# Decoding float64 weights: the sign by a Sign activation and a multiplication instead of a bit operation

## The chip, the cores and the metric

The kernel runs on one core of a Trainium2 chip, as one launch. Times are device microseconds (us) of that core, from the first instruction to the last result in memory. A profiled execution of each kernel gives a trace of every instruction. The engines are called PE (matrix multiplication), DVE (VectorE), ACT (ScalarE), POOL (GpSimd) and SP (which issues most transfers).

## The reference

Three stages follow one another. The first is attention with only the 32 largest scores of each row kept, over 4 batches, 8 heads, 576 positions, head size 64. The second is a feed-forward layer with softplus on 2304 tokens of 512, hidden size 2048. The third sends each token to one of 8 experts.

```python
scores = scale * np.matmul(q, k.transpose(0, 1, 3, 2))
kth = np.partition(scores, -top_k, axis=-1)[..., -top_k:-top_k + 1]
scores = np.where(scores >= kth, scores, -1000000000.0)
...
h = x @ w_in                                   # w_in: 512 x 2048, float64
g = np.maximum(h, 0.0) + np.log1p(np.exp(-np.abs(h)))
x = (g @ w_out).astype(np.float32)             # w_out: 2048 x 512, float64
...
expert_idx = np.argmax(x @ w_gate, axis=1)
ye = np.maximum(xe @ w1[e], 0.0) @ w2[e]       # per expert, scaled by its gate
```

The weights `w_in` and `w_out` of the second stage arrive as float64. The engines compute in float32, so the kernel has to decode them: each value is two 32-bit words, and the float32 is made from both.

## The kernel before

`part_one` does attention and the feed-forward layer, `part_two` the experts. Attention is cut into 72 groups of two score tiles of 128x576. For a group, PE makes the scores (line 394), ACT copies them (402), DVE finds the 32nd largest value by folding the row and by rounds of MAX and MATCH_REPLACE (430 to 454), ACT takes the exponential (443), the exponentials are multiplied by a mask (on POOL, 466, with the mask from DVE, 465; from group 12 on one of the two tiles is masked on DVE alone, 462), ACT makes a 16-bit copy (470), POOL subtracts to get the remainder (471, 472), a DMA transposes the result, and PE multiplies it by v three groups later (489, 491).

Once a tile of tokens has all its heads, the feed-forward layer takes it in units of up to two tiles, in 16 steps per unit: a first layer (576), the exponential and logarithm on ACT (590, 591), and a second layer (616). `some_work` starts 1.7 such steps per group, as far as units are ready.

The weights are decoded in 32 steps of 128x512 values, 16 of `w_in` and 16 of `w_out`, by `decode` (from line 225). Two steps are called ahead of group 0 and four behind each softmax, at the lowest priority; the scheduler that writes the order of every engine places them between the other work, so that they spread over some 20 groups. A step loads the words into `w` (two buffers), of which `hi` and `lo` are views with a stride of two words. With the buffer `a` (called `xr` in the trace, two buffers, shared with a later use) it does:

- line 233, ACT: the high word, read as a float, times 2 to the power of -111, into `a`;
- line 235, DVE: `a` shifted left by 3 bits, in place, which puts exponent and upper mantissa where a float32 has them, and drops the sign;
- line 237, ACT: the low word as an integer, scaled and rounded to the lowest bits, in place;
- line 238, DVE: the sign bit of the high word, or-ed into `a`;
- line 239, POOL: an integer addition of the low bits to `a`, into the target: `t` for `w_in`, `w_out_s` for `w_out`.

For `w_in`, ACT then makes a 16-bit copy of `t` (244, 245) and POOL the remainder (246). PE's first layer waits for these.

Of the kernel before, what the change touches and what calls it, by code (L numbers as in the profile page):

```python
# [8 lines left out]
F32 = mybir.dt.float32  # L9
F32R = mybir.dt.float32r  # L10
F16 = mybir.dt.float16
I32 = mybir.dt.int32
U32 = mybir.dt.uint32
AF = mybir.ActivationFunctionType
ALU = mybir.AluOpType
# [176 lines left out]
def part_one(tc, ctx, q, k, v, w_in, w_out, const, ident, before, ones, iota_e, reg_e, wg, ids,  # L192
             ohcum, done, early, table, rows, flags, sums, w_sums, e_sums):
    nc = tc.nc
# [30 lines left out]
    def decode(src, kk, c0, dst):  # L225
        w = dec.tile([128, 2 * C], I32, name="w", bufs=DWB)
        nc.sync.dma_start(w, src[:, kk, 2 * c0:2 * (c0 + C)])
        w = w.rearrange("p (a b) -> p a b", b=2)
        hi, lo = w[:, :, 1], w[:, :, 0]
        a = x2p.tile([128, ROWW], F32, name="xr")[:, :C]  # L230


        nc.scalar.activation(a, hi.bitcast(F32), AF.Copy, scale=2.0 ** -111)
        u = a.bitcast(U32)
        nc.vector.tensor_scalar(u, u, 3, None, op0=ALU.logical_shift_left)

        nc.scalar.activation(lo, lo.bitcast(U32), AF.Copy, scale=2.0 ** -29)
        nc.vector.scalar_tensor_tensor(u, hi.bitcast(U32), 0x80000000, u, op0=ALU.bitwise_and, op1=ALU.bitwise_or)  # L238
        nc.gpsimd.tensor_tensor(out=dst.bitcast(I32), in0=a.bitcast(I32), in1=lo, op=ALU.add)

    def decode_w_in(kk, j):
        t = dec.tile([128, C], F32, name="t")
        decode(w_in_v, kk, j * C, t)
        nc.scalar.activation(w_in_s[:, kk, j, 1], t, AF.Abs, accum_out=w_sums[:, j, kk:kk + 1])
        nc.scalar.activation(w_in_s[:, kk, j, 0], t, AF.Copy)
        nc.gpsimd.tensor_tensor(out=w_in_s[:, kk, j, 1], in0=t, in1=w_in_s[:, kk, j, 0], op=ALU.subtract)
# [39 lines left out]
    for j in range(DFF // C):  # L286
        if flags is None:
            dec_q += [(decode, w_in_v, kk, j * C, w_in_f[:, kk, j]) for kk in range(KD)]
            dec_q += [(split_w_in, j)]
        else:  # L290
            dec_q += [(decode_w_in, kk, j) for kk in range(KD)]
        dec_q += [(decode, w_out_v, kk, c0, w_out_s[:, kk, c0:c0 + C])
                  for kk in range(j * C // 128, (j + 1) * C // 128) for c0 in range(0, DM, C)]
# [791 lines left out]
```

## Time and profile before

| what | us |
|---|---|
| median of 3 runs | 1109.52 (1106.35 to 1110.75) |
| time of the profiled execution | 1105.04 |
| span of the profiled execution | 1103.2 |
| PE busy | 891.7 (81%) |
| DVE busy | 937.9 (85%) |
| ACT busy | 743.3 (67%) |
| POOL busy | 521.4 (47%) |

"Busy" is the time between an instruction's start and its end in the trace. It includes time in which a started instruction waits inside the engine. Idle time before an instruction is listed with the engine or transfer that ended it. The shares are means over the whole span; the stages differ a good deal, so the tables by window matter more than the mean.

### The profile page before, as it was taken

The numbers are of one execution on the slowest core, as the hardware profiler recorded it, in microseconds if no ns is written. First come the engines' busy times: TensorE is split into PE (matmuls) and PEld (weight loads), VectorE is DVE, ScalarE is ACT, GpSimd is POOL, SyncE is SP. The second block draws the span as 40 slices with busy tenths as digits, with TensorE's granted clock in tenths as the row PEclk, the third lists the DMA queues.
The fourth block names the chain that finished last, engine by engine and source line by source line (L and its number), as shares of the span: only waits on it lengthen the run. The fifth ranks groups of instructions, "written<-read, shape, count | busy, mean of one in ns | idle before, by whom it ended". The sixth has DMA issues, their size and how long they took to land.

```text
span 1103.2 us, 22060 instructions
## 1 busy us (share of the span) xinstructions
PE 891.7 (81%) x7146; PEld 648.0 (59%) x7146; DVE 937.9 (85%) x2989; ACT 743.3 (67%) x1738; POOL 521.4 (47%) x571
## 2 busy tenths in 40 slices
PE   1123259757978898799999898998999999999995
PEld 0012135434654564566556565666678899999994
DVE  4998999999977997999899999999746897777774
ACT  5757678777756776767787776775578655555553
POOL 2877988786535564654655554644301011211111
PEclk9998569858889999899999999999999999999998
DMA  7887698876656779644878645434621376566660
GB/s 178 207 155 169 159 202 162 186 184 128 117 94 104 138 123 155 134 78 81 143 147 141 106 91 83 85 76 75 176 67 30 98 249 210 206 245 236 219 230 24
DMA packets 295858, 156.96 MB, mean 142 GB/s; under 512 B 257524, under 2 KB 257652, under 8 KB 295732
## 3 DMA queue, kind: packets, MB, share of 16 engines
q1 hardware_dynamic: 292116, 145.73, 60.4%
q0 software_dynamic: 3616, 9.72, 2.5%
q8 instruction: 58, 0.95, 0.4%
q14 instruction: 68, 0.56, 0.2%
HBM read 77.89 MB, written 11.11 MB: 81 GB/s over the span
## 4 chain that ended last, share of the span: by engine, by line
PE 40%; DVE 27%; DMA 13%; issue 6%; ACT 5%; POOL 5%; SPq 3%; POOLq 0%; ACTq 0%; DVEq 0%
PE h L916 9%; PE y L929 9%; PE h L576 8%; DVE mx L454 6%; DVE wk L450 6%; PE y L616 5%; DMA pT<-p 5%; PE y L613 3%; DVE wk L446 2%; DVE mk L465 2%; DVE e L462 2%; POOL p L472 2%; DVE xr L238 2%; DMA kt<-st 2%; DMA qn<-in_q_dram 2%
## 5 line engine op out<-in xcount | busy, mean ns | idle before, releaser
L576 PE MATMUL h<-xT,w_in_s 128*128 128x256 f16 (+1 forms) x1920 | 227.2, 269 | 27.2 <-ACT sa L590 13.0
L616 PE MATMUL y<-w_out_s,g 128*128 128x512 f32 x480 | 233.2, 607 | 9.3 <-ACT g L591 9.3
L576 PEld LDWEIGHTS <-w_in_s 128*128 128x128 f16 x1920 | 173.6, 101 | 95.5 <-issue 63.6
L394 PE MATMUL s<-kt,q 128*128 128x512 f16 (+7 forms) x640 | 103.6, 327 | 137.1 <-DVE wk L446 90.5
L454 DVE MAX8 mx<-wk 128x8 f32<-128x144 f32 (+2 forms) x432 | 199.0, 495 | 0.1
L466 POOL TENSOR_TENSOR e<-e,mk 128x576 f32<-128x576 f32 x84 | 110.3, 1316 | 130.1 <-DVE mk L465 57.2
L472 POOL TENSOR_TENSOR p<-e,p 128x512 f16<-128x512 f32 x144 | 167.7, 1165 | 0.0
L470 ACT ACTIVATE p<-e 128x576 f16<-128x576 f32 x144 | 97.8, 679 | 94.4 <-DVE e L462 36.5
L394 PEld LDWEIGHTS <-q 128*128 128x128 f16 (+1 forms) x640 | 46.4, 110 | 190.6 <-DVE wk L446 76.7
L450 DVE MATCH_REPLACE8 wk<-mx,wk 128x144 f32<-128x144 f32 (+1 forms) x432 | 144.7, 341 | 0.1
L616 PEld LDWEIGHTS y<-w_out_s,g 128*128 128x128 f32 x480 | 82.2, 192 | 71.3 <-issue 55.2
L916 PEld LDWEIGHTS h<-xT,wf 128*128 128x128 f32 x864 | 111.8, 191 | 5.3 <-ACT wf L877 0.2
L916 PE MATMUL h<-xT,wf 128*128 128x256 f32 x864 | 113.9, 283 | 0.0
L929 PE MATMUL y<-wf,hT 128*128 128x512 f32 x432 | 112.9, 399 | 0.3 <-DVE ds L673 0.3
L443 ACT ACTIVATE e<-s,bias 128x576 f32<-128x576 f32 x144 | 105.0, 767 | 4.6 <-POOL p L472 2.9
L489 PE MATMUL m<-v,pT 128*128 128x65 f16 (+1 forms) x1440 | 96.4, 203 | 13.1 <-ACT xtail L517 5.8
L896 POOL DMA_INDIRECT out_dram<-ot,idx x19 | 19.6, 1029 | 176.1 <-DVE ot L895 173.4
L489 PEld LDWEIGHTS <-pT 128*128 128x128 f16 (+1 forms) x1440 | 89.5, 108 | 18.6 <-issue 14.7
L402 ACT ACTIVATE s<-s 128x1152 f32<-128x1152 f32 x72 | 80.4, 1117 | 11.3 <-PE s L394 11.2
L471 POOL TENSOR_TENSOR p<-e,p 128x64 f16<-128x64 f32 x144 | 51.0, 354 | 76.6 <-ACT p L470 74.4
L929 PEld LDWEIGHTS y<-wf,hT 128*128 128x128 f32 x432 | 76.7, 189 | 13.4 <-DVE ds L673 0.3
L491 PE MATMUL m<-v,pT 128*128 128x64 f16 (+1 forms) x800 | 78.5, 203 | 0.0
(197 smaller groups left out, 1752.5 us busy)
## 6 DMA issues: line engine op xcount, KB each, us to landing
w1r<-in_moe_w_dram SPq DMA_DIRECT2D x20, 1024.0 KB, 4.9
w2r<-in_moe_w_dram SPq DMA_DIRECT2D x20, 1024.0 KB, 7.6
w<-in_moe_w_in_dram SPq DMA_DIRECT2D x16, 512.0 KB, 5.0
w<-in_moe_w_out_dram SPq DMA_DIRECT2D x16, 512.0 KB, 4.0
rows<-xr SPq DMA_DIRECT2D x37, 128.2 KB, 2.5
qn<-in_q_dram SPq DMA_DIRECT2D x16, 288.0 KB, 4.5
kn<-in_k_dram SPq DMA_DIRECT2D x16, 288.0 KB, 3.0
vn<-in_v_dram SPq DMA_DIRECT2D x16, 288.0 KB, 4.5
```

Source lines behind the costliest of these rows:

```text
L394: last_qk[0] = nc.tensor.matmul(ps[p0:p1, base + k0 * D:base + k1 * D], lhsT=lhs, rhs=kt[:, k0:k1, cs], start=first, stop=not first)
L443: nc.scalar.activation(e[i], s[i], AF.Exp, bias=bt[:, i], scale=SCORE if flags is not None else sc[i][:, 3:4])
L450: nc.vector.match_replace(out=to, in_to_replace=mx[:, i, 8 * j:8 * j + 8], in_values=src[i], imm_value=NEG)
L454: nc.vector.max(out=mx[:, i, 8 * j + 8:8 * j + 16], in_=src[i])
L466: nc.gpsimd.tensor_tensor(out=e[i], in0=e[i], in1=mk, op=ALU.mult)
L470: nc.scalar.activation(p16[:, 0:S], e[i], AF.Copy)
L472: nc.gpsimd.tensor_tensor(out=p16[:, S + D:], in0=e[i][:, 0:S - D], in1=p16[:, 0:S - D], op=ALU.subtract)
L489: nc.tensor.matmul(o[:, h, 0:D + 1], lhsT=pT(r), rhs=v16[:, h, c, 0:D + 1], start=r == 0, stop=r == R - 1)
L576: nc.tensor.matmul(hps[:, :n], lhsT=w_in_s[:, c, j, p, o:o + 128], rhs=xT[:, 0:len(u.tiles), r, c, :], start=m == 0, stop=m == 3 * KD - 1)
L616: nc.tensor.matmul(u.y[i], lhsT=g[:, cs], rhs=w_out_s[:, f, :], start=f == 0, stop=f == KF - 1)
L916: nc.tensor.matmul(h, lhsT=w1f[:, a, c, :], rhs=xT[:, b, c, :], start=n == 0, stop=n == 3 * KD - 1)
L929: nc.tensor.matmul(y[i], lhsT=hT[g][:, a, i * 128:i * 128 + 128], rhs=w2f[:, b, :], start=g == 0 and n == 0, stop=g == KF2 - 1 and n == 2)
```

## The change

Line 233 takes the magnitude (Abs) in place of a copy, a new ACT instruction turns the high word into its sign as a float (-1 or 1), in place, the addition writes to `a`, and a second POOL instruction multiplies `a` by the sign into the target. The DVE instruction of line 238 is gone. From line 238 on, line numbers are one higher: 239 is the addition, 240 the multiplication, 238 the Sign.

```diff
-        nc.scalar.activation(a, hi.bitcast(F32), AF.Copy, scale=2.0 ** -111)
+        nc.scalar.activation(a, hi.bitcast(F32), AF.Abs, scale=2.0 ** -111)
         u = a.bitcast(U32)
         nc.vector.tensor_scalar(u, u, 3, None, op0=ALU.logical_shift_left)
 
         nc.scalar.activation(lo, lo.bitcast(U32), AF.Copy, scale=2.0 ** -29)
-        nc.vector.scalar_tensor_tensor(u, hi.bitcast(U32), 0x80000000, u, op0=ALU.bitwise_and, op1=ALU.bitwise_or)
-        nc.gpsimd.tensor_tensor(out=dst.bitcast(I32), in0=a.bitcast(I32), in1=lo, op=ALU.add)
+        nc.scalar.activation(hi.bitcast(F32), hi.bitcast(F32), AF.Sign)
+        nc.gpsimd.tensor_tensor(out=a.bitcast(I32), in0=a.bitcast(I32), in1=lo, op=ALU.add)
+        nc.gpsimd.tensor_tensor(out=dst, in0=a, in1=hi.bitcast(F32), op=ALU.mult)
```

The scheduler writes a new order for every engine. On POOL, at softmax groups 6 and 7 (`e` are the exponentials, `mk` the masks, `p_...` the 16-bit copies of one tile), the order was before:

```order
L466 TENSOR_TENSOR e<-e,mk 128x576 x2
L471 TENSOR_TENSOR p_1075<-e,p_1075 128x64
L472 TENSOR_TENSOR p_1075<-e,p_1075 128x512
L239 TENSOR_TENSOR t<-xr,w 128x512
L471 TENSOR_TENSOR p_1081<-e,p_1081 128x64
L472 TENSOR_TENSOR p_1081<-e,p_1081 128x512
L246 TENSOR_TENSOR w_in_s<-t,w_in_s 128x512
L239 TENSOR_TENSOR t<-xr,w 128x512
L466 TENSOR_TENSOR e<-e,mk 128x576
L246 TENSOR_TENSOR w_in_s<-t,w_in_s 128x512
L466 TENSOR_TENSOR e<-e,mk 128x576
```

And with the change, at the same two groups:

```order
L467 TENSOR_TENSOR e<-e,mk 128x576
L239 TENSOR_TENSOR xr<-xr,w 128x512
L240 TENSOR_TENSOR t<-xr,w 128x512
L467 TENSOR_TENSOR e<-e,mk 128x576
L472 TENSOR_TENSOR p_1101<-e,p_1101 128x64
L473 TENSOR_TENSOR p_1101<-e,p_1101 128x512
L247 TENSOR_TENSOR w_in_s<-t,w_in_s 128x512
L472 TENSOR_TENSOR p_1107<-e,p_1107 128x64
L473 TENSOR_TENSOR p_1107<-e,p_1107 128x512
L467 TENSOR_TENSOR e<-e,mk 128x576
L240 TENSOR_TENSOR t<-xr,w 128x512
L467 TENSOR_TENSOR e<-e,mk 128x576
```

Where a group had two decoding steps between its subtractions, there is now about one per group, and it is two instructions, which stand between the group's multiplications by the mask.

On DVE, the last decoding step stood before in softmax group 19 (`wk` and `mx` are the row being searched and its largest values):

```order
L450 MATCH_REPLACE wk<-mx,wk 128x144 x2
L235 TENSOR_SCALAR xr<-xr 128x512
L515 RECIPROCAL rc<-rc 64x2
L454 MAX mx<-wk 128x8 x2
L238 SCALAR_TENSOR_TENSOR xr<-w,xr 128x512
```

With the change it stands at the end of group 24, ahead of the first line of group 25:

```order
L466 TENSOR_SCALAR mk<-s,mx 128x576
L463 SCALAR_TENSOR_TENSOR e<-s,mx,e 128x576
L235 TENSOR_SCALAR xr<-xr 128x512
L604 TENSOR_TENSOR w<-w_out_s,w 128x512
L431 TENSOR_TENSOR s<-s 128x288
```

The 32 steps now reach five groups further. In ACT's order, counted by the score copies (402) issued ahead of it, the feed-forward layer's 12th step came after 17 groups and now comes after 19, the 24th after 26 and now 28, the 36th after 32 and now 35, the 48th after 38 and now 40, the 96th after 59 in both. ACT's orders hold one load of an activation table each, at the start. The number of transfers is the same.

## Rows read from the trace of the kernel before

**Rows 1.** Page, part 2: busy tenths of 40 slices, PE, DVE and POOL.

```profile
PE   1123259757978898799999898998999999999995
...
DVE  4998999999977997999899999999746897777774
...
POOL 2877988786535564654655554644301011211111
```

**Rows 2.** Windows of the span; columns start:end, length, then busy us (instructions) by engine.

```profile
42.00:176.00 134.00, 52.78 (x467) 34.10 (x468) 129.53 (x358) 94.61 (x194) 113.99 (x106) 0.81 0.82 176
176.00:262.00 86.00, 62.37 (x482) 37.46 (x481) 82.13 (x233) 67.56 (x158) 64.38 (x63) 0.78 0.80 173
262.00:307.00 45.00, 35.20 (x307) 24.11 (x306) 44.83 (x165) 31.46 (x69) 25.77 (x31) 0.85 0.65 120
307.00:440.00 133.00, 112.59 (x921) 72.31 (x920) 110.49 (x395) 87.87 (x215) 67.75 (x77) 0.96 0.73 120
440.00:765.00 325.00, 300.19 (x2721) 200.19 (x2722) 309.85 (x1131) 236.34 (x587) 174.37 (x207) 0.98 0.59 104
765.00:1103.00 338.00, 322.10 (x2230) 277.41 (x2228) 236.06 (x646) 199.91 (x470) 55.89 (x57) 0.99 0.50 164
```

**Rows 3.** Line L238 and, up to 308 us, line L430: xcount, duration ns min/median/max, first and last.

```profile
L238 DVE SCALAR_TENSOR_TENSOR xr<-w,xr x32: 662/1316/1754, 11.0 to 256.9; 128x512 uint32<-128x512 uint32 x32
...
L430 DVE TENSOR_TENSOR s<-s x26: 436/450/467, 22.9 to 306.5; 128x288 f32<-128x288 f32 x26
```

**Rows 4.** Waits of DVE, 42 to 176 us: us in total, times, longest.

```profile
DVE xr L235 <- ACT xr L233: 3.2, 3, 1.6
DVE s L430 <- ACT s L402: 1.2, 1, 1.2
```

**Rows 5.** Timeline, 105.9 to 110 us, DVE and POOL: start, us, engine, line.

```profile
105.95 0.68 DVE L238 SCALAR_TENSOR_TENSOR xr<-w,xr 128x512 uint32<-128x512 uint32 x1
107.11 1.57 DVE L238 SCALAR_TENSOR_TENSOR xr<-w,xr 128x512 uint32<-128x512 uint32 x1
...
106.98 1.16 POOL L472 TENSOR_TENSOR p<-e,p 128x512 f16<-128x512 f32 x1
108.10 1.73 POOL L239 TENSOR_TENSOR t<-xr,w 128x512 int32<-128x512 int32 x1
```

**Rows 6.** Duration of one, lines L235, L446, L239 and L472: xcount, ns min/median/max.

```profile
L235 DVE TENSOR_SCALAR xr<-xr x32: 401/604/1514, 10.5 to 256.0; 128x512 uint32<-128x512 uint32 x32
...
L446 DVE TENSOR_TENSOR wk<-s x72: 740/748/751, 24.7 to 765.1; 128x576 f32<-128x576 f32 x72
...
L239 POOL TENSOR_TENSOR t<-xr,w x16: 1275/1290/1809, 11.8 to 235.2; 128x512 int32<-128x512 int32 x16
...
L472 POOL TENSOR_TENSOR p<-e,p x144: 1147/1159/1367, 37.8 to 777.3; 128x512 f16<-128x512 f32 x144
```

**Rows 7.** Groups of instructions by line and form: busy us, mean ns, idle before.

```profile
L238 DVE SCALAR_TENSOR_TENSOR xr<-w,xr 128x512 uint32<-128x512 uint32 x32 | 38.6, 1205 | 0.1
L235 DVE TENSOR_SCALAR xr<-xr 128x512 uint32<-128x512 uint32 x32 | 24.9, 778 | 7.9 <-ACT xr L233 7.9
...
L239 POOL TENSOR_TENSOR t<-xr,w 128x512 int32<-128x512 int32 x16 | 22.5, 1408 | 10.3 <-DVE xr L238 10.0
...
L233 ACT ACTIVATE xr<-w 128x512 f32<-128x512 f32 x32 | 21.3, 665 | 27.8 <-DMA w<-in_moe_w_in_dram 12.2 <-DMA w<-in_moe_w_out_dram 11.7 <-POOL e L466 2.9
```

**Rows 8.** Windows with line L238 alone: 42 to 176, 176 to 262, and their sum.

```profile
42.00:176.00 134.00, 18.78 (x16) 0.81 0.82 176
176.00:262.00 86.00, 14.57 (x12) 0.78 0.80 173
...
sum 265.00, DVE 33.35; mean DVE 11.12
```

**Rows 9.** Window of 20 us in which POOL was fullest, and the first 42 us.

```profile
0.00:42.00 42.00, 6.44 (x24) 2.39 (x24) 25.00 (x67) 25.55 (x50) 19.25 (x32) 1.00 0.80 185
...
120.00:140.00 20.00, 4.45 (x43) 2.66 (x44) 20.00 (x54) 12.48 (x24) 18.82 (x17) 0.56 0.75 169
```

**Rows 10.** Waits of POOL, 42 to 176 us, the longest.

```profile
POOL p L471 <- ACT p L470: 6.6, 6, 2.6
POOL e L466 <- DVE mk L465: 5.6, 12, 0.8
```

**Rows 11.** Chain of waits, 324 to 328 us, PE: one step of the first unit.

```profile
324.78 1.72 PE y L616 x4
326.50 1.31 PE h L576 x12
```

**Rows 12.** Groups by line: the one table load of ScalarE.

```profile
L95 ACT ACT_TABLE_LOAD x1 | 1.3, 1283 | 0.8 <-PEq L1067 0.8
```

## The prediction, made before the changed kernel was run

> **What bounds the kernel now.** I first read the busy slices of the page [rows 1]. They show three stages: from about 40 to 300 us DVE is full while PE is far from full; from 300 to about 770 us both are near full; after that PE is full. The change is in the first stage only, since line L238 runs from 11.0 to 256.9 us [rows 3]. So the second view is a table of windows, with cuts at the last decoding steps: between 42 and 307 us DVE is busy 129.53 + 82.13 + 44.83 = 256.5 of 265 us, POOL 113.99 + 64.38 + 25.77 = 204.1, ACT 94.61 + 67.56 + 31.46 = 193.6 [rows 2]. The end at 307 is the start of softmax group 25 (line L430 starts its 26th group, counted from 0, at 306.5) [rows 3]; the new order issues the last decoding step there, so it is the place where both kernels have done the same work. The third view, the waits of DVE, says who releases whom: from 42 to 176 us DVE waits 3.2 and 1.2 us for others and for nothing else worth a row [rows 4]. Read alone, that makes DVE the bound, and any DVE work taken away a gain.
>
> The fourth view corrects this. L238 lasts from 662 to 1754 ns, median 1316 [rows 3], for one shape. In the timeline the one at 105.95 us, with no POOL instruction running, takes 0.68 us; the one at 107.11 takes 1.57, and POOL's L472 runs until 108.14 beneath it, so that it ends 0.54 us after L472. POOL's next, an L239, starts at 108.10 and takes 1.73 us [rows 5] where its shortest is 1.275 [rows 6]. So these two engines hold each other up: DVE's "busy" hides waiting for POOL. L235 shows it too (401 to 1514 ns); L446, of which one operand lies in PSUM, does not (740 to 751) [rows 6]. The work that passes through one gate in this stage is POOL's, plus some DVE instructions.
>
> **The change, part by part.** *Removed:* 32 L238, 38.6 us of DVE, mean 1205 ns [rows 7]; 28 of them, 33.35 us, lie after 42 us [rows 8]. Own work in that is 28 x 0.662 = 18.5 us; the rest, 14.8, is waiting. DVE's demand up to group 25 falls to 256.5 - 33.35 = 223.1 us at most, and L235 and L465 will wait longer if POOL is fuller.
>
> *Added on POOL:* 32 float multiplications of 128x512, 28 of them in the stretch. No row shows this one. Below it stands L472 (float, one operand of 16 bits, 1147 shortest, 1159 median), above it the mean of L239, 1408, which has its own holds in it [rows 6, 7]. I take L239's median, 1290, since it has the same tiles, two operands of 4 bytes and one of them with a stride: 28 x 1.29 = 36.1 us, bounds 28 x 1.16 = 32.5 and 28 x 1.408 = 39.4.
>
> *Relief on POOL:* an L238 held the next POOL instruction up by 1.73 - 1.275 = 0.455 us [rows 5, 6]. Bounds: 0 and 28 x 0.455 = 12.7 us. As more than half of the L238 last twice their shortest time, most met a POOL instruction; I take two thirds, 8.5 us. So POOL's demand up to group 25 is 204.1 + 36.1 - 8.5 = 231.7 us (bounds 224 and 243.5), more than DVE's 223.1. POOL becomes the fuller engine.
>
> The Trainium skill (SBUF — State Buffer, "Who interferes with whom") says that a DVE instruction with two SBUF inputs contends with GpSimd reads, and in a two-port mode whichever comes first keeps the shared pair for the whole instruction, the other blocking fully. For who contends, the trace agrees. If the hold were the whole L238, the relief would be 28 x 0.662 = 18.5 us and POOL's demand 221.7; the row above shows 0.455, and the sum goes by that.
>
> *Added on ACT:* 32 Sign activations of the shape of L233, 665 ns [rows 7]: 28 x 0.665 = 18.6 us, ACT to 212 of 265, 80%. I cost it at nothing, since ACT would still have 53 us idle. Without that cover it reaches POOL through the copies L470, for which POOL already waits 6.6 us between 42 and 176 [rows 10]. Abs for Copy on L233 and the addition written to `xr` change no shape: nothing.
>
> *The added wait:* the multiplication stands on POOL behind the addition and waits for the Sign. Queued behind it are the softmax's e-multiplication and the p-subtractions, and after them the transposes, the L470 copies and DVE's next mask (two `mk` buffers). The `w` and `xr` buffers, two each, are held one multiplication longer, 1.29 us and its place in the queue; no load is added, but SP issues them with it. The order spreads the steps over five more groups, which covers this; without that cover it is 28 x 1.29 / 2 = 18 us.
>
> *The first 42 us:* POOL is busy 19.25 of 42 us [rows 9]; four steps lose an L238 and gain a multiplication in its place: nothing.
>
> **The sum.** What share of its time can POOL be busy? In the long dense stretch it was 113.99 of 134 us, 85.1% [rows 2]; in its fullest 20 us 18.82, 94% [rows 9]. I take 85.1%, because POOL's waits there, for L470 and for the mask [rows 10], are still there: 231.7 / 0.851 = 272.3 us instead of 265, **+7.3 us**. The ends: 231.7 / 0.94 = 246 (-19), and 243.5 / 0.851 = 286 (+21).
>
> *Behind group 25* the first-layer steps are late: by the new order the 12th and 24th are issued two groups later, the 36th three, the 96th at the same group. Three groups are some six steps of 1.31 + 1.72 = 3.03 us of PE [rows 11], 18 us, to be fitted into PE's idle time from 307 to 765 us, (133 - 112.6) + (325 - 300.2) = 45 us [rows 2]. Bounds 0 and 18; since the idle time is two and a half times that, I take **+2 us**. Together +9.3 on the profiled execution's 1105.0 us gives 1114.3; the median of the runs shown, 1109.5, stands 4.5 above that execution, so the forecast is **1119 us**.
>
> **Rivals.**
> - *DVE was the bound and POOL keeps up* (the other side). For it: DVE is 97% busy and hardly waits [rows 2, 4], and 33.35 us go. Against it: 14.8 us of those were waiting for POOL, and POOL's load grows. It decides if POOL can run at 94% through the whole stretch, as in its best 20 us: -19 us, 1090. With DVE at 223.1 us and no waits it would be -33 at the very most. Chance 0.23.
> - *Even exchange:* POOL at 87 to 89% (231.7 / 0.88 = 263), because DVE, relieved, delivers masks earlier; or the hold was a whole L238, as the page's rule has it: 221.7 / 0.851 = 260.5, -4.5, with +2 behind: 1107. Between 1104 and 1115. Chance 0.27.
> - *The late steps are not absorbed:* PE is 92% busy from 440 to 765 us, 300.19 of 325 [rows 2], so all 18 us could come out at the end on top of the 7: 1109.5 + 25 = 1135. Chance 0.07.
> - *Sign needs another table:* a load is 1283 ns [rows 12]; two for each of 32 steps are 82 us of ACT, above 1150. Against it: both orders hold one load, at the start. Chance 0.02.
>
> **How the numbers follow.** My forecast has 0.41, its own range 1115 to 1136. What lies within 0.5%, about what a measurement of this kernel can tell from no change, is 1104 to 1115. Slower: 0.41 + 0.07 + 0.02 = 0.50; same 0.27; faster 0.23. The range reaches down to the first rival's price, 1091, beyond which some 0.08 is left, and up to 1138, which takes in the third rival and most of the upper bound (1109.5 + 21 + 2 = 1132), with some 0.08 beyond.
>
> **What would show it.** Right: POOL above 225 us busy up to the 26th L430 and that one later than 307 us; L235's mean above its 778 ns; DVE with idle time that ends on POOL or on ACT's L470; the multiplication near 1.29 us. Wrong: the 26th L430 before 300 us with POOL at 90% or more; a multiplication near 0.9 us; DVE still full; or a group 25 on time and a late end.

## The result, and the profile after

The changed kernel takes 1115.57 us, median of 12 runs (1111.35 to 1118.61), against 1106.88 us for the kernel before, also 12 runs (1101.63 to 1110.75). The ratio is 1.0072, 95% interval 1.0049 to 1.0094: slower by some 8 us, and the interval leaves out no change. The forecast was 1119 us and slower. The profiled execution took 1116.81 us, 11.8 us more than that of the kernel before (1105.04); a comparison of the two traces has these 11.8 us to explain, not 8.

The direction and the size came out; two terms of the sum did not, and by luck their errors cancelled. The windows of the changed kernel, with the cuts of [rows 2] (start:end, length, then busy us and instructions of PE, weight loads, DVE, ACT and POOL; the last window is longer by the 12 us between the two profiled executions):

```profile
42.00:176.00 134.00, 54.78 (x488) 35.95 (x488) 122.70 (x371) 98.06 (x202) 125.65 (x121) 0.77 0.78 168
176.00:262.00 86.00, 57.30 (x483) 34.22 (x482) 83.97 (x246) 73.86 (x165) 81.26 (x79) 0.78 0.88 187
262.00:307.00 45.00, 30.85 (x213) 18.89 (x212) 40.55 (x116) 32.96 (x72) 35.68 (x36) 0.75 0.49 113
307.00:440.00 133.00, 118.62 (x980) 76.83 (x980) 110.64 (x411) 89.23 (x224) 70.79 (x81) 0.97 0.88 131
440.00:765.00 325.00, 303.25 (x2671) 202.20 (x2670) 296.05 (x1087) 229.16 (x577) 167.60 (x197) 0.97 0.61 100
765.00:1115.00 350.00, 331.22 (x2294) 283.05 (x2292) 241.81 (x662) 203.92 (x479) 58.46 (x59) 0.98 0.50 159
```

POOL is now busy 125.65 of 134 us and 81.26 of 86, 94% in both; before it was 85 and 75%. PE's busy time from 42 to 307 us fell from 52.78 + 62.37 + 35.20 = 150.4 to 142.9 us. The next rows show softmax group 25 (the 26th start of the first folding line), the multiplication, and the shift; the columns are count, shortest/median/longest duration in ns, first and last start in us.

```profile
L431 DVE TENSOR_TENSOR s<-s x26: 436/453/467, 19.9 to 295.4; 128x288 f32<-128x288 f32 x26
...
L240 POOL TENSOR_TENSOR t<-xr,w x16: 1284/1307/1824, 12.3 to 267.9; 128x512 f32<-128x512 f32 x16
L240 POOL TENSOR_TENSOR w_out_s<-xr,w x16: 1279/1302/1522, 58.4 to 297.8; 128x512 f32<-128x512 f32 x16
...
L235 DVE TENSOR_SCALAR xr<-xr x32: 402/691/1494, 10.4 to 292.1; 128x512 uint32<-128x512 uint32 x32
```

Group 25 starts at 295.4 us, where it was 306.5 [rows 3]: **earlier** by 11 us, where I had it 7 us later. The multiplication lasts 1302 to 1307 ns, near the 1290 I took. The shift's median rose from 604 [rows 6] to 691 ns, its mean from 778 [rows 7] to 802.

The relief of DVE did not arrive whole. The first row below is the changed kernel from 42 us to its group 25 (columns as above). The others are the mask instruction of DVE over the same groups, up to 306.5 us before and 295.4 us after (count, then busy us and mean ns):

```profile
42.00:295.00 253.00, 134.87 (x1148) 84.97 (x1148) 238.24 (x702) 197.14 (x422) 235.73 (x226) 0.77 0.78 169
...
L465 DVE TENSOR_SCALAR mk<-s,mx 128x576 f16<-128x576 f32 x34 | 26.0, 771 | 0.0
...
L466 DVE TENSOR_SCALAR mk<-s,mx 128x576 f16<-128x576 f32 x34 | 34.9, 1033 | 0.3
```

DVE was busy 256.5 us for this work before [rows 2], and now 238.2: 18 us less, although 33.35 us of line 238 are gone. The mask alone took back some 9 of the other 15, its mean risen from 771 to 1033 ns for one shape.

What POOL waited for changed too. Before, it waited from 42 to 176 us for the copies (6.6 us) and for the masks (5.6 us) [rows 10]. The waits of POOL in the changed kernel, for the same stretch, the three longest and the one for the mask (us in total, times, longest):

```profile
POOL xr L239 <- issue: 2.5, 3, 1.6
POOL xr L239 <- ACT w L237: 1.9, 1, 1.9
POOL xr L239 <- ACT x L518: 1.2, 1, 1.2
...
POOL e L467 <- DVE mk L466: 0.9, 2, 0.5
```

With one more instruction per step, and the decoding placed between the multiplications by the mask, POOL has other work while a mask or a copy is late, and its old waits all but vanish. I had assumed that they stay.

The loss appears later. The next rows are the first 24 exponentials of the feed-forward's first layer in the kernel before (the last start, 320.3, is the 24th step), with its last addition for `w_out`, started at 258.2 us:

```profile
L590 ACT ACTIVATE sa<-h x24: 358/374/396, 162.1 to 320.3; 128x256 f32<-128x256 f32 x24
...
L239 POOL TENSOR_TENSOR w_out_s<-xr,w x16: 1277/1294/1741, 50.9 to 258.2; 128x512 int32<-128x512 int32 x16
```

In the changed kernel the last multiplication starts at 297.8 us (the `w_out_s` row above), 40 us later, and the 24th step 9 us later:

```profile
L591 ACT ACTIVATE sa<-h x24: 361/367/392, 164.2 to 329.6; 128x256 f32<-128x256 f32 x24
```

PE waited for that last multiplication, which it did not do in the kernel before. In the waits of PE from 262 to 310 us (us in total, times, longest) the changed kernel has:

```profile
PE y L617 <- POOL w_out_s L240: 3.9, 1, 3.9
```

So attention is 11 us ahead at group 25 and the feed-forward layer 9 us behind, and the program ends late. The next rows carry both streams to their ends, before and after: the first folding line of all 72 groups, whose last start is the last group's, and the exponentials of all 160 feed-forward steps, whose last start is the last step's.

```profile
L430 DVE TENSOR_TENSOR s<-s x72: 436/454/467, 22.9 to 761.4; 128x288 f32<-128x288 f32 x72
...
L590 ACT ACTIVATE sa<-h x160: 253/367/407, 162.1 to 861.7; 128x256 f32<-128x256 f32 x128, 128x128 f32<-128x128 f32 x32
...
L431 DVE TENSOR_TENSOR s<-s x72: 436/456/467, 19.9 to 767.0; 128x288 f32<-128x288 f32 x72
...
L591 ACT ACTIVATE sa<-h x160: 253/366/398, 164.2 to 873.2; 128x256 f32<-128x256 f32 x128, 128x128 f32<-128x128 f32 x32
```

Attention's lead is gone by its last group, 5.6 us late, and the last feed-forward step is 11.5 us late, all but 0.3 us of the difference between the two profiled executions. From the last step to the end of the span it is 241.5 us before and 241.8 after. The experiments ask which of these decides, and what each part of the change is worth.

### The profile page after: what moved, and what is told of

Same layout as the page of the kernel before. It is cut to its first block, busy times and chain, and to the rows that moved or that the text cites. A ratio compares the mean times of both kernels' runs of the same rounds, so it can differ in the third digit from the quotient of the medians.

```text
span 1115.0 us, 22063 instructions
## 1 busy us (share of the span) xinstructions
PE 902.4 (81%) x7146; PEld 653.5 (59%) x7146; DVE 918.8 (82%) x2957; ACT 755.5 (68%) x1770; POOL 561.8 (50%) x603
## 4 chain that ended last, share of the span: by engine, by line
PE 34%; DVE 29%; DMA 16%; ACT 8%; issue 5%; POOL 5%; SPq 3%; POOLq 0%; ACTq 0%; DVEq 0%
PE h L917 9%; PE y L930 9%; DVE mx L455 6%; DMA pT<-p 6%; DVE wk L451 6%; PE h L577 5%; PE y L614 3%; PE y L617 3%; DVE mk L466 3%; DVE e L463 2%; DVE wk L447 2%; DMA w<-in_moe_w_in_dram 2%; DMA q<-st 2%; POOL p L473 2%; DVE xr L235 2%
## 5 line engine op out<-in xcount | busy, mean ns | idle before, releaser
L577 PE MATMUL h<-xT,w_in_s 128*128 128x256 f16 (+1 forms) x1920 | 231.0, 271 | 23.1 <-ACT sa L591 17.9
L577 PEld LDWEIGHTS <-w_in_s 128*128 128x128 f16 x1920 | 175.9, 102 | 90.3 <-issue 61.9
L395 PE MATMUL s<-kt,q 128*128 128x512 f16 (+7 forms) x640 | 107.2, 332 | 135.5 <-DVE wk L447 76.9
L490 PE MATMUL m<-v,pT 128*128 128x65 f16 (+1 forms) x1440 | 99.8, 205 | 24.0 <-ACT x L518 15.8
L472 POOL TENSOR_TENSOR p<-e,p 128x64 f16<-128x64 f32 x144 | 50.6, 352 | 75.1 <-ACT p L471 74.1
```

The lines of the kernel that those rows point to most:

```text
L395: last_qk[0] = nc.tensor.matmul(ps[p0:p1, base + k0 * D:base + k1 * D], lhsT=lhs, rhs=kt[:, k0:k1, cs], start=first, stop=not first)
L490: nc.tensor.matmul(o[:, h, 0:D + 1], lhsT=pT(r), rhs=v16[:, h, c, 0:D + 1], start=r == 0, stop=r == R - 1)
L577: nc.tensor.matmul(hps[:, :n], lhsT=w_in_s[:, c, j, p, o:o + 128], rhs=xT[:, 0:len(u.tiles), r, c, :], start=m == 0, stop=m == 3 * KD - 1)
```

## The experiments

Three theories: **late steps** (a decoding step holds its two buffers longer, the weights come late, and PE has more left); **gate** (POOL's added time, shared with DVE, sets the time wherever the steps stand); **order** (the scheduler wrote a new order, and any new order moves the time by this much). Each ratio is to the kernel before on the same chip, with its 95% interval.

Two things hold for all the expectations. They count softmax groups from 1, so that their groups 20 and 25 are 19 and 24 elsewhere here. And where they give a time for the feed-forward layer's 12th step, it is 245 to 290 us, too late by some 40 us or more: the step starts at 207.9 us before, at 220.5 in the changed kernel, 205.7 in decode_first, 226.8 in long_hold, 206.3 in no_addition and 216.3 in before_decode_first. Only which of them come earlier or later came out, and for the last not even that.

### decode_first: the same instructions, the steps earlier

```diff
-            with tc.high_priority(offset=0):
+            with tc.high_priority(offset=400):
                 decode_some(DECR)
```

> The changed kernel, with the decoding steps given precedence over the softmax when the order is written; the instructions are the same, but the last step stands in group 22 instead of 25, the feed-forward layer's 12th step after 17 score copies instead of 19 (17 before the change). Late steps (the changed kernel loses because a step holds its two buffers longer, the weights come later and PE has more left): the 12th step starts near 250 us instead of 280, ratio to before 0.995 to 1.002. Gate (POOL's added 36 us set the time): the same POOL work, denser, 1.007 or more. Order (any new order moves the time by chance): anything from 1.000 to 1.012, with no link to the 12th step.

Measured: 0.9959 (0.9928 to 0.9990), 1103.2 us. The rows below are the 24th feed-forward step, the last multiplication, the 25 starts up to group 24 and the first two windows:

```profile
L591 ACT ACTIVATE sa<-h x24: 362/384/418, 161.9 to 312.3; 128x256 f32<-128x256 f32 x24
...
L240 POOL TENSOR_TENSOR w_out_s<-xr,w x16: 1283/1308/1802, 30.7 to 266.4; 128x512 f32<-128x512 f32 x16
...
L431 DVE TENSOR_TENSOR s<-s x25: 439/450/467, 22.2 to 283.1; 128x288 f32<-128x288 f32 x25
...
42.00:176.00 134.00, 52.89 (x497) 35.26 (x498) 120.64 (x354) 99.85 (x207) 128.54 (x123) 0.73 0.78 175
176.00:262.00 86.00, 63.78 (x520) 38.42 (x519) 83.24 (x252) 74.01 (x169) 79.64 (x79) 0.82 0.86 180
```

Group 24 starts at 283.1 us; in the changed kernel it was 282.8. But the 24th step starts at 312.3 instead of 329.6, and the last multiplication at 266.4 instead of 297.8. POOL does the same work at the same density (128.54 + 79.64 of 220 us, 95%), PE no longer waits for the last multiplication, and the program is some 12 us faster than the changed kernel (0.9959 against 1.0072), and faster than before. The gate alone is out.

### before_decode_first: the control

The kernel before with a precedence too, but with 1500 in place of 0 where decode_first has 400; the expectation's "same precedence" is of the kind, not of the size.

> The kernel before, with the same precedence for the decoding steps as in decode_first; the last step stands in group 17 instead of 20, the 12th step still after 17 score copies. It is the control of decode_first. Late steps: 12th step at the same time or up to 10 us earlier, ratio 0.990 to 1.000. Gate and order: 0.995 to 1.005.

Measured: 1.0034 (1.0006 to 1.0061). The precedence is no gain by itself; the expectation from late steps (0.990 to 1.000) was missed, although the 24th step came 8 us earlier here too; its 12th step came 8 us later. With 400, the kernel before was not run.

### long_hold: the lateness without the work

```diff
         nc.gpsimd.tensor_tensor(out=dst.bitcast(I32), in0=a.bitcast(I32), in1=lo, op=ALU.add)
+        hold = sm.tile([128, 1], F32, name="hold")
+        nc.vector.tensor_tensor(out=hold, in0=dst[:, 0:1], in1=hi.bitcast(F32)[:, 0:1], op=ALU.add)
+        nc.gpsimd.tensor_tensor(out=hold, in0=hold, in1=hi.bitcast(F32)[:, 0:1], op=ALU.add)
```

> The kernel before, with two tiny instructions behind each addition that read one column of the buffers (DVE, then POOL), so that a step holds its buffers as long as in the changed kernel; the order then has the last step in group 25 and the 12th, 24th and 36th steps after 19, 28 and 34 score copies, as the changed kernel has (19, 28, 35). Work added: 32 times some 0.2 us on DVE and POOL. Late steps: the 12th step starts at 270 to 290 us, and the ratio to before is 1.006 to 1.02. Gate: no POOL work to speak of is added, 1.000 to 1.004.

Measured: 1.0050 (1.0024 to 1.0077). The rows: the 24th step, the last addition for `w_out`, and the added DVE instruction on one column.

```profile
L593 ACT ACTIVATE sa<-h x24: 359/372/398, 155.9 to 331.5; 128x256 f32<-128x256 f32 x24
...
L239 POOL TENSOR_TENSOR w_out_s<-xr,w x16: 1276/1284/1507, 49.9 to 302.3; 128x512 int32<-128x512 int32 x16
...
L241 DVE TENSOR_TENSOR hold<-w_out_s,w x16: 135/304/1232, 54.3 to 305.2; 128x1 f32<-128x1 f32 x16
```

The last addition starts at 302.3 instead of 258.2 us and the 24th step at 331.5 instead of 320.3, as late as in the changed kernel, with 32 tiny instructions on each of two engines. The ratio stands a little under the range that late steps gave and above that of the gate. Lateness and the added instructions together thus cost some 5 us. The latter are busy for 14.1 us on DVE and 8.7 on POOL, so that the share of lateness alone is not shown; but PE waits for one of the last additions of `w_out_s` here too (1.3 us, until 300.7 us).

### no_addition: DVE relieved, POOL not loaded

```diff
-        nc.gpsimd.tensor_tensor(out=a.bitcast(I32), in0=a.bitcast(I32), in1=lo, op=ALU.add)
```

> The changed kernel without the integer addition of the low bits, so that the weights lack their last bits: DVE is relieved as in the change, ACT has the Sign, and POOL has one instruction per step, as before the change. Late steps: the step is shorter by one POOL instruction and its place in the queue, the last stands in group 23, the 12th starts near 245 to 260 us, ratio 0.990 to 1.000. Gate: POOL has 36 us less and DVE 33 us less than in the respective kernels, so that the stretch up to group 25 takes 25 us less than before, and the end 20 us, ratio 0.975 to 0.985.

Measured: 0.9745 (0.9712 to 0.9779), 1078.8 us. The starts up to group 24, the 24th step, and the windows up to 262 us:

```profile
L430 DVE TENSOR_TENSOR s<-s x25: 440/452/467, 22.3 to 274.6; 128x288 f32<-128x288 f32 x25
...
L590 ACT ACTIVATE sa<-h x24: 362/382/443, 160.2 to 304.6; 128x256 f32<-128x256 f32 x24
...
42.00:176.00 134.00, 55.70 (x532) 36.23 (x533) 123.87 (x384) 106.10 (x219) 114.46 (x113) 0.72 0.82 180
176.00:262.00 86.00, 60.02 (x505) 37.83 (x503) 84.60 (x256) 79.49 (x181) 72.98 (x73) 0.76 0.94 194
```

Group 24 at 274.6 us (298 before) and the 24th step at 304.6: both early. This is the gate's forecast, by a hair below its range, and not that of late steps. Relieving DVE of line 238 **is** worth 28 us, and POOL's second instruction then takes some 36 us back (1.0072 against 0.9745). With the steps early, as in decode_first, it still takes 24 (0.9959 against 0.9745). So lateness is not the whole story either.

### extra_mult and sign_only: POOL's and ACT's part alone

extra_mult, in the kernel before:

```diff
-        nc.gpsimd.tensor_tensor(out=dst.bitcast(I32), in0=a.bitcast(I32), in1=lo, op=ALU.add)
+        nc.gpsimd.tensor_tensor(out=a.bitcast(I32), in0=a.bitcast(I32), in1=lo, op=ALU.add)
+        nc.gpsimd.tensor_tensor(out=dst, in0=a, in1=ones[:, 0:1].to_broadcast([128, C]), op=ALU.mult)
```

> The kernel before with a second POOL instruction per step, a multiplication by one, while the bit operation of line 238 stays on DVE and ACT stays as it was: POOL's part of the change alone. If POOL's instruction costs what no_addition gave back (1115.6 to 1078.8, 37 us), the ratio to before is 1.02 to 1.035. If only the lateness of the decoding steps costs (as in long_hold; the last stands in group 24 here), 1.004 to 1.010.

sign_only, in the kernel before, in front of the addition:

```diff
+        nc.scalar.activation(hi.bitcast(F32), hi.bitcast(F32), AF.Sign)
```

> The kernel before with the Sign activation added behind line 238, its result used by nothing: ACT's part of the change alone, 32 times 0.67 us, with the last step in group 22. If ACT has room, 0.998 to 1.004; if ACT's queue holds up the copies for POOL, 1.005 to 1.015.

Measured: extra_mult 1.0086 (1.0053 to 1.0118), sign_only 1.0020 (0.9992 to 1.0048). ACT's part is within what can be measured. POOL's second instruction costs 0.9% where DVE keeps its own, far less than the 2 to 3.5% that I expected from no_addition, and within the range that I gave for lateness alone; PE waits for the last multiplication here too (1.7 us). It is also a cheaper instruction than the change's, 1041 ns at the median against 1302 to 1307; it reads one column of ones over and over in place of the strided words, and is busy 36.5 us in 32 steps against 43.2. The windows of extra_mult up to 262 us fit with the small price:

```profile
42.00:176.00 134.00, 54.76 (x498) 36.02 (x499) 133.66 (x379) 90.49 (x188) 124.67 (x118) 0.69 0.76 168
176.00:262.00 86.00, 54.40 (x436) 32.59 (x434) 85.58 (x236) 66.28 (x146) 79.30 (x78) 0.74 0.80 175
```

DVE is at 133.66 of 134 us and POOL at 124.67: DVE stays the full engine, and POOL, 81% busy there in the kernel before (113.99 + 64.38 of 220), still had some for the multiplication.

### mult_on_dve and no_pool: the work moved the other way

mult_on_dve, in the changed kernel:

```diff
-        nc.gpsimd.tensor_tensor(out=dst, in0=a, in1=hi.bitcast(F32), op=ALU.mult)
+        nc.vector.tensor_tensor(out=dst, in0=a, in1=hi.bitcast(F32), op=ALU.mult)
```

> The changed kernel with the multiplication by the sign on DVE instead of POOL: DVE 2 instructions per step, POOL 1, ACT 3, and the order of sign_only. If the number of instructions on DVE and POOL decides, and not their kind, it stands with sign_only (1.002): 0.999 to 1.005. If Abs, Sign and the multiplication cost by themselves: 1.006 to 1.012 like the changed kernel.

no_pool, in the kernel before (the bias cuts off the low bits instead of rounding them):

```diff
-        nc.vector.tensor_scalar(u, u, 3, None, op0=ALU.logical_shift_left)
-        nc.scalar.activation(lo, lo.bitcast(U32), AF.Copy, scale=2.0 ** -29)
-        nc.vector.scalar_tensor_tensor(u, hi.bitcast(U32), 0x80000000, u, op0=ALU.bitwise_and, op1=ALU.bitwise_or)
-        nc.gpsimd.tensor_tensor(out=dst.bitcast(I32), in0=a.bitcast(I32), in1=lo, op=ALU.add)
+        nc.scalar.activation(lo, lo.bitcast(U32), AF.Copy, scale=2.0 ** -29, bias=-0.5)
+        nc.vector.scalar_tensor_tensor(u, u, 3, lo.bitcast(U32), op0=ALU.logical_shift_left, op1=ALU.bitwise_or)
+        nc.vector.scalar_tensor_tensor(dst.bitcast(U32), hi.bitcast(U32), 0x80000000, u, op0=ALU.bitwise_and, op1=ALU.bitwise_or)
```

> The kernel before with the same shift and or, and the sign put in by DVE straight into the target: DVE 2 instructions of at least 0.66 us, POOL none, ACT 2. The last step stands in group 18. If the gate between POOL and DVE sets the time in the decoding stage, 36 us of it are taken away and 8 added: 0.975 to 0.99. If DVE's own work sets it, 1.000 to 1.008.

Measured: mult_on_dve 1.0002 (0.9975 to 1.0028), no_pool 1.0007 (0.9974 to 1.0040). The new instructions cost nothing by their kind; the engine that they stand on decides. And taking POOL out of the decoding altogether gains nothing as long as DVE has two instructions per step, though POOL's busy time falls to 97.47 and 49.57 us (113.99 and 64.38 in [rows 2]), while DVE stays full. That is what I expected if DVE's own work sets the time:

```profile
42.00:176.00 134.00, 48.62 (x449) 32.04 (x450) 129.01 (x363) 97.80 (x198) 97.47 (x91) 0.71 0.80 180
176.00:262.00 86.00, 62.78 (x505) 38.77 (x504) 85.39 (x251) 69.52 (x161) 49.57 (x54) 0.84 0.73 169
```

This is no pure removal: DVE's first instruction per step is now one of two inputs. The two of all steps are busy 64.5 us, as line 235 and line 238 were before (24.9 + 38.6 = 63.5 us [rows 7]), so that DVE was not relieved.

### or_low and or_low_first: one instruction on each

or_low, in the changed kernel; or_low_first adds the edit of decode_first:

```diff
-        nc.vector.tensor_scalar(u, u, 3, None, op0=ALU.logical_shift_left)
-        nc.scalar.activation(lo, lo.bitcast(U32), AF.Copy, scale=2.0 ** -29)
+        nc.scalar.activation(lo, lo.bitcast(U32), AF.Copy, scale=2.0 ** -29, bias=-0.5)
+        nc.vector.scalar_tensor_tensor(u, u, 3, lo.bitcast(U32), op0=ALU.logical_shift_left, op1=ALU.bitwise_or)
         nc.scalar.activation(hi.bitcast(F32), hi.bitcast(F32), AF.Sign)
-        nc.gpsimd.tensor_tensor(out=a.bitcast(I32), in0=a.bitcast(I32), in1=lo, op=ALU.add)
         nc.gpsimd.tensor_tensor(out=dst, in0=a, in1=hi.bitcast(F32), op=ALU.mult)
```

> The changed kernel with the low bits cut off (by a bias of -0.5) and put in by the DVE shift, as one instruction with a shift and a bitwise or, so that POOL's addition is not needed: DVE 1 instruction of at least 0.66 us, POOL 1, ACT 3. The last step stands in group 21, the 12th step after 17 score copies. If POOL's second instruction is what eats the gain, the ratio is 0.975 to 0.99, a few us above no_addition (0.9745) because DVE's instruction is 0.26 us longer. If the moved load does not matter and only the new order does, 0.995 to 1.005.

> or_low with the precedence for decoding steps of decode_first; the last step stands in group 18 instead of 21. If early steps pay wherever neither DVE nor POOL is overfull, as between the changed kernel and decode_first (12 us), the ratio to before is 0.975 to 0.988. If precedence only helps where the steps were late (before_decode_first: 1.0034), 0.988 to 0.995.

Measured: or_low 0.9895 (0.9835 to 0.9955), 1099.4 us; or_low_first 0.9856 (0.9822 to 0.9889), 1093.8 us, which beats both kernels. or_low gains, though at the edge of its range and 15 thousandths less than no_addition; its DVE instruction reads two buffers and takes 667 ns at the shortest, the plain shift 401 [rows 6], so it relieves DVE less. or_low_first came out as expected if early steps pay.

### order_after and order_before: what a new order alone does

The edit of decode_first with 60 in place of 400, in the changed kernel and in the kernel before.

> The changed kernel with a small precedence (60 in place of 400), by which the order of every engine is written anew, but the decoding steps stand as late as before (last step in group 26, 12th feed-forward step after 19 score copies): a control for what a new order alone does. If the lateness of the steps is what decode_first mended: 1.005 to 1.011, as the changed kernel. If new orders scatter by as much as decode_first gained: anywhere from 0.995 to 1.015.

> The kernel before with the same small precedence: its order is written anew, the last step stands in group 20 as before. The other control: 0.997 to 1.003 if new orders alone do little.

Measured: order_after 1.0105 (1.0068 to 1.0142), order_before 1.0009 (0.9985 to 1.0034). A new order with the steps where they were does not mend the changed kernel, and does nothing to the kernel before; these are two orders, and how far others scatter is not shown. order_after is telling in another way; its starts up to group 24, and its 24th step:

```profile
L431 DVE TENSOR_TENSOR s<-s x25: 436/448/467, 20.3 to 275.3; 128x288 f32<-128x288 f32 x25
...
L591 ACT ACTIVATE sa<-h x24: 361/376/407, 162.7 to 339.9; 128x256 f32<-128x256 f32 x24
```

Its group 24 starts at 275.3 us, as early as in no_addition, yet it is the slowest of all; its 24th step comes at 339.9, and PE waits 2.4 us for the last multiplication.

### All of them side by side

The columns DVE and POOL are instructions per step. "Group 24", "24th step", "last group" and "last step" are starts in us in the profiled execution, from the rows shown for the named kernels and from the same lines of the others.

| kernel | DVE | POOL | group 24 | 24th step | last group | last step | ratio |
|---|---|---|---|---|---|---|---|
| before | 2 | 1 | 298 | 320 | 761 | 862 | 1 |
| no_addition | 1 | 1 | 275 | 305 | 734 | 834 | 0.9745 |
| or_low_first | 1 | 1 | 283 | 302 | 751 | 850 | 0.9856 |
| or_low | 1 | 1 | 282 | 311 | 755 | 854 | 0.9895 |
| decode_first | 1 | 2 | 283 | 312 | 761 | 860 | 0.9959 |
| changed | 1 | 2 | 283 | 330 | 767 | 873 | 1.0072 |
| order_after | 1 | 2 | 275 | 340 | 769 | 879 | 1.0105 |
| mult_on_dve | 2 | 1 | 292 | 306 | 763 | 865 | 1.0002 |
| no_pool | 2 | 0 | 293 | 315 | 769 | 870 | 1.0007 |
| order_before | 2 | 1 | 297 | 311 | 770 | 870 | 1.0009 |
| sign_only | 2 | 1 | 295 | 317 | 775 | 875 | 1.0020 |
| before_decode_first | 2 | 1 | 294 | 312 | 764 | 864 | 1.0034 |
| long_hold | 3 (one tiny) | 2 (one tiny) | 294 | 332 | 762 | 868 | 1.0050 |
| extra_mult | 2 | 2 | 298 | 337 | 770 | 879 | 1.0086 |

Read by the first two starts, the table falls into three parts. Where group 24 stays at 292 us or later and the 24th step between 306 and 320, the ratio is 1.000 to 1.003. Where group 24 comes at 275 to 283 **and** the 24th step at 312 or before, it is 0.975 to 0.996. Where the 24th step comes at 330 or later, it is 1.005 to 1.011, whether group 24 is early or not. A gain went with attention and the feed-forward layer both early; a late feed-forward layer alone was enough to lose.

The last two starts say how. From the last step to the end of the span it is 241.1 to 242.5 us in all fourteen, so what differs comes before. From the last group to the last step it is 98 to 102 us in ten of them. In the other four (changed, order_after, long_hold, extra_mult) it is 106 to 110, and these are the four in which PE waits for weights of `w_out` from POOL near 300 us. decode_first, the changed kernel's instructions with early steps, is back at 99. The time of a kernel is thus the end of attention plus what the feed-forward layer then still has to do, and where the weights are late the second is some 6 to 10 us longer. Each start is of one execution, and executions of one kernel differ by more than 1%, so that small differences between rows of one column mean little.

The clock granted to PE is no rival: its mean, as a share of full speed, is 0.933 in the profiled execution of no_addition, the fastest, and 0.935 in that of order_after, the slowest.

## Why the prediction came out, and which steps of it failed

- **What bounds the stage: half right.** DVE's busy time held waiting for POOL, L235 and the mask waited longer as foretold, and POOL's demand up to group 25 was well forecast: 235.7 us against 231.7. But DVE is as full beside it (both 94% of 42 to 262 us), and in the kernel before it is DVE's time, waits included, that counts, not POOL's work as the prediction concludes: with one instruction on POOL, relieving DVE brought 28 us (no_addition); with two on DVE, taking POOL's away brought nothing (no_pool, whose DVE instructions are no shorter in all). Only with two on POOL does relieving DVE bring little: 1.0086 (extra_mult, whose multiplication is shorter) to 1.0072 in the orders as the scheduler wrote them; extra_mult with early steps was not run.
- **The multiplication at 1.29 us: right** (1302 to 1307). **The Sign at nothing: right** within the interval of sign_only.
- **"I take 85.1%, because POOL's waits there ... are still there": the first failed step.** The waits for the copies and masks went, and POOL ran at 94% through 220 us, not only through its best 20 (93% up to group 25). So group 25 came 11 us earlier instead of 7 us later. That is the mechanism of my first rival; its price, -19 us, was nearer than mine.
- **"The order spreads the steps over five more groups, which covers this": the second failed step.** The spreading is no cover, it is how the longer hold shows. Before, the last addition started at 258.2 us, and with the change the last multiplication at 297.8, and PE waited for it. I had named the uncovered price, 18 us, and put it aside.
- **"I take +2 us" behind group 25: the third**, mis-sized. From 11 us ahead at group 25 to 8 us behind at the end are some 19 us lost on the way, about the 18 of my upper bound. The feed-forward layer was not caught up in PE's idle time: it was 12.6 us late at its 12th step, before group 25, and still 11.5 us late at its last. PE was busy 118.62 + 303.25 + 331.22 = 753.1 of the 808 us from 307 us on, 93%, as the third rival had it. Of the profiled 11.5 us, 5.8 are the longer way from the last group to the last step (100.3 to 106.1 us), which long_hold shows as well (106.5). The other 5.6 are attention's own, which went from 11 us early at group 25 to 5.6 late at its last group; what took these 17 us is not shown.
- The sum, +9.3, came out by luck: the first error (18 us too slow) and the third (17 us too fast) cancelled. Two of the signs that I listed under wrong came true: group 25 before 300 us with POOL at 90% or more, and a group 25 on time with a late end. Of those under right, POOL's busy time, the multiplication and the shift's mean came true; a group 25 later than 307 us and idle time of DVE that ends on POOL did not.
- *A reading:* that "more than half" of the L238 lasted twice their shortest time is a little too much. Twice 662 is 1324 ns, above the median of 1316 [rows 3]; it was half of them.
- **The rule of the Trainium skill** (SBUF — State Buffer, "Who interferes with whom"), by which the relief on POOL would be larger, can't be judged by the end time, since POOL's share moved more than the relief. POOL's busy time up to group 25, 235.7 us, is nearer to my 231.7 than to the 221.7 that I worked out for the whole hold, but waits on other DVE instructions are in it too. On the waiting itself the trace of long_hold agrees with it: a DVE instruction on one column with two SBUF inputs lasted from 135 to 1232 ns.

## What to carry to other kernels

When two engines share a gate, test relief in a table of two by two: here DVE's relief was worth 28 us with one POOL instruction per step and almost nothing with two, and what it is worth with two depends on the order as well (decode_first). An engine's busy share in its densest stretch is no ceiling, because its waits shrink when it has more to do; look at what it waits for and whether new work can stand there. A longer path through a pair of buffers is a delay of all that needs the result, even when the added instructions are tiny (long_hold): find the consumer. And where one stream follows another to the program's end, follow both through to their last step: a lead halfway is no gain yet.

## What was not expected of the hardware

One column can wait as long as a whole tile: the added DVE instruction of long_hold, 135 ns at its shortest, had a median of 304 and a longest of 1232 ns for 128x1 elements, 1.1 us over its shortest, as the longest L238 is over its own (1754 over 662 [rows 3]). Its median waits less, 0.17 us against 0.65. POOL kept up a busy share of 94% over 220 us with DVE at 94% as well (122.70 + 83.97 of 220), although the two hold each other up. A multiplication of floats and an addition of integers, each with one operand at a stride of two words, take POOL the same time (1302 to 1307 and 1290 ns); with one column read over and over in place of the strided operand, the multiplication took 1041 ns (extra_mult).
